# Amplitude product of kernel generation in two halves, with amplitudes in two tiles and new instruction sequences

## The chip, the cores and the metric

The kernel runs on one core of a Trainium2 chip. The core has a matrix engine (TensorE, PE in the profile, with its weight loads as PEld), three engines for elementwise work (VectorE, DVE; ScalarE, ACT; GpSimd, POOL) and a queue that issues the transfers (SyncE, SP). Each engine runs its own list of instructions in order and waits on semaphores for the others. The metric is the device time of one execution in microseconds, median of some runs.

## The reference

The input is a sequence of 2048 positions with 448 channels. Two branches work on it and a gate mixes them. Branch a is a state space model (S4D): per channel a convolution kernel K of length 2048 is generated from 256 complex modes, and the sequence is convolved with K by FFT. Branch b is a gated unit with 1792 features.

```python
x = A_u                                             # (1, 2048, 448)
g = sigmoid((x * gate_w).sum(-1, keepdims=True))

dt = exp(log_dt)
A = -exp(log_A_real) + 1j * A_imag                  # (448, 256)
C = (C_real + 1j * C_imag) * dt[:, None]
P = exp((A * dt[:, None])[:, :, None] * pos)        # (448, 256, 2048)
K = 2.0 * einsum("dn,dnl->dl", C, P).real           # kernel generation
y = irfft(rfft(x, 4096) * rfft(K, 4096))[:2048]
a = y + x * D_skip

b = (sigmoid(B_x_in @ w_gate) * (B_x_in @ w_up)) @ w_down    # B_x_in is x
out = g * a + (1 - g) * b
```

P would have 448 x 256 x 2048 entries; the kernel never forms it.

## The kernel before, in words

**Kernel generation.** A position is written as l = 32 a + b, and exp(A dt l) as a product of a factor in a and one in b, so that K is, per channel, a small matrix product over the modes. The 448 channels are worked in 28 chunks of 16 (`kgen`), the modes in two halves of 128, one on each partition: 56 half chunks. For each, `powers` lets POOL build tables of real powers (tile `tb`; L1212 sets ones, L1222 and L1225 multiply), and `half_chunk` makes the factors: PE computes phases in turns (L1232), ACT and PE take the whole turns off (L1236, L1238 and L1241), ACT makes sines and cosines (L1243, L1244, L1254) in the tile `cs` of 96 columns for each of sine and cosine and each of 16 channels. DVE makes the amplitudes `es` (96 columns) as two outer products of the small tables (L1261: 64 columns, 1024 elements a partition, then 32 columns, 512 elements) and multiplies them into cs: L1275 writes the columns 0 to 31 of cs from its columns 32 to 63 in reversed order and the first 32 of es (the part called n here, 1024 elements), and L1278 multiplies columns 32 to 95 in place by es 32 to 95 (2048 elements). `contract` then multiplies both half chunks of a chunk together on PE (L1290: 128 small matmuls of 32 columns), ACT takes the result out, and after 14 chunks the kernel of one half of the channels goes to memory for the FFT.

**The other work.** The gated unit runs for each of two halves of the positions in two blocks of 512. Its weights are split in two parts of less precision (`wh`, `wl`: ACT L1388, DVE or POOL L1390), so that one product is three matmuls (L1423 to L1425, and L1427, L1428 for the shorter last part) into PSUM tiles `gu`. ACT makes the tanh of the gate (L1407) and DVE the product (L1409, or L1412 and L1415 where it is split again into `hh` and `hl`). The down product goes to a PSUM tile `dn`, of which there is one (L1443; L1445 to L1447 where split), and from there into an output block `ob`: the first time by ACT (L1455) or DVE scaled by `og`, later by DVE adding (L1462). The gate's factors come from DVE: 16 dot products (L960), tanh on ACT, then `gs` = g (L964) and `og` = (1 - g)/2 (L966). FFT stages of the signal and of K are matmuls with DVE transposes and products between them.

**What sets the order.** The program lists its operations with what each reads and writes. A planner then emits them in an order that a table written into the kernel, `PLACE`, gives: for each engine, tile tag and priority a row of numbers, one for each operation, its place in that engine's list. Each engine's instructions run in the order of these places, SP's transfers too. A tile's buffers are handed out in rotation (`cs` 3, `tb` 2, `es` 1), so an operation that opens a new tile waits for the last user of the old one.

The lines of the diff, before:

## Time and profile before

| | us |
|---|---|
| runs | 687.88, 686.38, 685.76 (median 686.38) |
| profiled execution | 684.96 |
| its span, first to last instruction | 683.0 |
| PE busy | 669.7 (98%) |
| DVE busy | 603.7 (88%) |
| ACT busy | 509.7 (75%) |
| POOL busy | 269.2 (39%) |
| mean granted TensorE clock | 0.999 |

The busy time of an engine is the sum of what its instructions cover, so overlapping instructions count once. A row of a group has the line, the engine, the operation, what it writes and reads, the shapes and the count; behind the bars stand the total and mean time and the idle time of the engine before these instructions, with what ended it. A row of the timeline begins with start and duration in microseconds; brackets at its end give the idle time before it and its releaser. PE's matmuls are pipelined, so their records overlap by design. Kernel generation fills the stretch from about 75 to 500 us; the gated unit runs beside it all the time and alone with the second FFT chains after it.

### The profile page before, as it was taken

What the parts mean: (1) busy time and instruction counts of PE and PEld (TensorE: products, weight loads), DVE (VectorE), ACT (ScalarE), POOL (GpSimd) and SP (SyncE); (2) the same over time, 40 slices, a digit from 0 to 9 for tenths busy, and PEclk for the clock granted to TensorE, in tenths of its full rate; (3) what the DMA queues carried; (4) which work ended last, traced back from release to release, by engine and by line L of the source; (5) the groups of instructions that cost most, each with busy time, mean ns of one, the idle gap of its engine ahead of it and who ended that gap; (6) DMA issues with size and microseconds to landing.
All of it is one profiled execution on the core that took longest, in us unless ns stands there. A gap on an engine that the chain in (4) does not pass through costs nothing.

```text
span 683.0 us, 16235 instructions
## 1 busy us (share of the span) xinstructions
PE 669.7 (98%) x6568; PEld 480.6 (70%) x6568; DVE 603.7 (88%) x699; ACT 509.7 (75%) x928; POOL 269.2 (39%) x280
## 2 busy tenths in 40 slices
PE   8899999999999999999989999999999999999997
PEld 7677667877886687776646666778878766546864
DVE  7998999999899999999998999999974379667976
ACT  6588799898999999999999999999842442333110
POOL 0506486555466656675856567643000000000000
PEclk9999999999999999999999999999999999999999
DMA  8869432683793999737977884343968981888855
GB/s 265 222 146 245 111 101 57 174 217 139 208 173 85 204 203 225 237 111 178 176 211 179 200 212 113 124 155 111 204 133 217 280 292 66 300 276 217 153 141 129
DMA packets 96898, 122.79 MB, mean 180 GB/s; under 512 B 31032, under 2 KB 80504, under 8 KB 95800
## 3 DMA queue, kind: packets, MB, share of 16 engines
q1 hardware_dynamic: 96824, 121.76, 69.7%
q8 instruction: 52, 0.85, 0.5%
q14 instruction: 22, 0.18, 0.1%
HBM read 78.16 MB, written 43.58 MB: 178 GB/s over the span
## 4 chain that ended last, share of the span: by engine, by line
PE 82%; DVE 10%; ACT 3%; DMA 2%; issue 2%; SPq 1%; DVEq 0%
PE gu_gps L1423 10%; PE gu_gps L1424 9%; PE gu_gps L1425 9%; PE kp_egp L1290 7%; PE dn_gps L1443 6%; PE dn_gps L1445 5%; PE tp_egp L1232 4%; PE tp_egp L1241 4%; PE dn_gps L1446 4%; PE dn_gps L1447 4%; PE fps_fups L812 3%; PE gu_gps L1427 3%; PE fps_fups L845 3%; PE gu_gps L1428 3%; PE fps_fups L889 2%; PE fps_fkps L889 2%
## 5 line engine op out<-in xcount | busy, mean ns | idle before, releaser
L1423 PE MATMUL gu_gps<-xs_glu,wh_glu 128*128 128x512 f32 x336 | 144.6, 430 | 1.6 <-DVE hl_glu L1409 0.8
L1278 DVE TENSOR_TENSOR cs_eg<-cs_eg,es_eg 128x2048 f32<-128x2048 f32 x56 | 131.5, 2349 | 1.4
L1424 PE MATMUL gu_gps<-xs_glu,wh_glu 128*128 128x512 f32 x336 | 132.0, 393 | 0.1
L1425 PE MATMUL gu_gps<-xs_glu,wl_glu 128*128 128x512 f32 x336 | 131.7, 392 | 0.0
L1222 POOL TENSOR_TENSOR tb_eg<-tb_eg 128x96 f32<-128x96 f32 (+2 forms) x84 | 118.8, 1416 | 6.1
L1261 DVE TENSOR_TENSOR es_eg<-tb_eg 128x1024 f32<-128x1024 f32 x112 | 110.4, 1013 | 2.1 <-POOL tb_eg L1222 0.5
L1423 PEld LDWEIGHTS gu_gps<-xs_glu,wh_glu 128*128 128x128 f32 x336 | 63.2, 188 | 30.8 <-issue 15.8
L1275 DVE TENSOR_TENSOR cs_eg<-cs_eg,es_eg 128x1024 f32<-128x1024 f32 x56 | 70.8, 1264 | 8.2 <-ACT cs_eg L1254 5.8
L1238 ACT ACTIVATE nn_eg<-cs_eg 128x512 fp32r<-128x512 f32 x112 | 74.9, 669 | 3.8 <-PE tp_egp L1241 2.6
L1407 ACT ACTIVATE sg_glu<-gu_gps 128x512 f32<-128x512 f32 x56 | 34.5, 615 | 55.2 <-PE gu_gps L1428 54.9
L1424 PEld LDWEIGHTS gu_gps<-xs_glu,wh_glu 128*128 128x128 f32 x336 | 63.3, 188 | 16.0 <-issue 5.0
L1425 PEld LDWEIGHTS gu_gps<-xs_glu,wl_glu 128*128 128x128 f32 x336 | 63.1, 188 | 14.4
L1243 ACT ACTIVATE cs_eg<-tp_egp 128x512 f32<-128x512 f32 x112 | 70.0, 636 | 3.1 <-PE tp_egp L1241 2.7
L1236 ACT ACTIVATE cs_eg<-tp_egp 128x512 f32<-128x512 f32 x112 | 69.9, 633 | 2.7 <-PE tp_egp L1232 1.0
L1244 ACT ACTIVATE cs_eg<-tp_egp 128x512 f32<-128x512 f32 x112 | 69.0, 627 | 1.1 <-PE tp_egp L1241 1.1
L1254 ACT ACTIVATE cs_eg<-cs_eg,half_pi 128x1024 f32<-128x1024 f32 x56 | 66.7, 1191 | 0.2
L1225 POOL TENSOR_TENSOR tb_eg<-tb_eg,bs_eg 128x32 f32<-128x32 f32 x84 | 62.6, 745 | 6.4
L1462 DVE SCALAR_TENSOR_TENSOR ob_glu<-dn_gps,og,ob_glu 128x448 f32<-128x448 f32 x70 | 47.4, 677 | 16.0 <-PE dn_gps L1447 15.1
L1290 PEld LDWEIGHTS kp_egp<-cs_eg 128*32 128x32 f32 x3584 | 51.3, 110 | 10.7 <-issue 7.6
L1212 POOL MEMSET tb_eg<- 128x96 f32 x28 | 8.0, 287 | 127.9 <-DVE es_eg L1261 124.8
L1290 PE MATMUL kp_egp<-cs_eg 128*32 128x64 f32 x3584 | 55.8, 220 | 0.0
L1241 PE MATMUL tp_egp<-nn_eg,idn 128*128 128x512 f32 x112 | 51.4, 459 | 1.2 <-ACT nn_eg L1238 1.2
(168 smaller groups left out, 1326.0 us busy)
## 6 DMA issues: line engine op xcount, KB each, us to landing
shf<-fx_fu SPq DMA_DIRECT2D x16, 896.0 KB, 5.4
fx_fu<-shf SPq DMA_DIRECT2D x16, 896.0 KB, 10.4
us<-fx_fu SPq DMA_DIRECT2D x16, 896.0 KB, 9.7
xr_glu<-in_w_dram SPq DMA_DIRECT2D x46, 256.0 KB, 6.1
uax_fk<-us SPq DMA_DIRECT2D x16, 448.0 KB, 4.3
ua_fk<-us SPq DMA_DIRECT2D x16, 448.0 KB, 6.0
xr_glu<-in_w_dram SPq DMA_DIRECT2D x17, 224.0 KB, 4.1
gt_pre<-in_u_dram SPq DMA_DIRECT2D x8, 448.0 KB, 6.9
```

The lines of the kernel that those rows point to most:

```text
L1222: pool(96 * m, lambda n=n, m=m: G.tensor_mul(g3(n + 1, m), g3(1, m), g3(n, 1).to_broadcast([128, 32, 3, m])))
L1236: op("Act", c_act(512, True), lambda: S.activation(cs[:, 1, ds, 32:96], block(tp), AF.Copy, bias=MAGIC), [tp], [(cs, ("s", i))], prio)
L1238: op("Act", c_act(512), lambda: S.activation(block(nn), cs[:, 1, ds, 32:96], AF.Copy, scale=-1.0, bias=MAGIC), [(cs, ("s", i))], [nn], prio)
L1241: op("PE", c_mm(532), lambda: T.matmul(tp.real, idn.real, nn.real, start=False, stop=True, skip_group_check=True), [nn, idn], [tp], prio)
L1243: op("Act", c_act(512, True), lambda: S.activation(cs[:, 0, ds, 32:96], block(tp), AF.Abs), [tp], [(cs, ("c", i))], prio)
L1261: V.tensor_mul(o.rearrange("p d (i k) -> p d i k", k=ny), x.unsqueeze(3).to_broadcast([128, 16, nx, ny]), y.unsqueeze(2).to_broadcast([128 ...
L1275: op("DVE", c_dve(1024), lambda: V.tensor_mul(cs[:, :, :, 0:32], cs[:, ::-1, :, 63:31:-1], es[:, :, 0:32].unsqueeze(1).to_broadcast([128, ...
L1278: op("DVE", c_dve(2048), lambda: V.tensor_mul(cs[:, :, :, 32:96], cs[:, :, :, 32:96], es[:, :, 32:96].unsqueeze(1).to_broadcast([128, 2, 1 ...
L1290: T.matmul(kp[32 * j:32 * j + 32, q], cs[:, z, 4 * j + q, 64:96], cs[:, z, 4 * j + q, 0:64], start=cs is parts[0] and z == 0 and q == 0, s ...
L1423: T.matmul(p.real, wh[:, k, cs], x[:, k], start=(k == 0), stop=False)
L1424: T.matmul(p.real, wh[:, k, cs], x[:, 4 + k], start=False, stop=False)
L1425: T.matmul(p.real, wl[:, k, cs], x[:, k], start=False, stop=False)
```

## The change

Two things change. First, `half_chunk`: the amplitudes are now two tiles, `ea` for the first 64 columns and `es` (called eb in the code) for the last 32, one buffer each, of the same size together. The product of 2048 elements becomes two of 1024: f, columns 64 to 95 of cs by es (L1279), and m, columns 32 to 63 by the second half of ea (L1282). The part n (now L1276) reads the columns that m overwrites, so m comes after n; f needs neither. Lines below this part stand four further down in the changed kernel (L1423 is L1427 there), those above it two.

Second, `PLACE`: every row of it has new numbers, with 168 numbers for the operations on cs in place of 112 on DVE, and a row for ea. So the sequence of every engine is another, also where the operations are the same. The diff of the code, with the first numbers of the rows for cs as an example of the table:

```diff
-    ('DVE', 'cs', 20): (156, 158, 168, 169, 180, 186, 192, 193, 201, 202, 206, 208, 215, 217, 221, 223, 228, 229, 233,
...
+    ('DVE', 'cs', 20): (157, 156, 159, 166, 168, 171, 182, 192, 188, 193, 196, 195, 204, 205, 206, 210, 211, 212, 220,
...
@@ -1246,7 +1248,7 @@
 
     def half_chunk(c, nh, ph, tb, prio):
         cs = eg.tile("cs", CSB, (128, 2, 16, 96))
-        es = eg.tile("es", 1, (128, 16, 96))
+        ea, eb = eg.tile("ea", 1, (128, 16, 64)), eg.tile("es", 1, (128, 16, 32))
         for i in range(2):
             tp = egp.tile("tp", TPB, (128, 512))
             turns(c, nh, i, ph, cs, tp, prio)
@@ -1265,19 +1267,21 @@
         def r(k):
             tt = tb[:, q0:q0 + 16]
             if k == 0:
-                outer(es[:, :, 0:64], tt[:, :, 8:16], tt[:, :, 0:8])
+                outer(ea.real, tt[:, :, 8:16], tt[:, :, 0:8])
             else:
-                outer(es[:, :, 64:96], tt[:, :, 24:28], tt[:, :, 16:24])
+                outer(eb.real, tt[:, :, 24:28], tt[:, :, 16:24])
         for k in range(2):
-            op("DVE", c_dve(1024 - 512 * k), lambda k=k: r(k), [tb], [(es, 0), (es, 1)] if k == 0 else [(es, 2)], prio)
-
+            op("DVE", c_dve(1024 - 512 * k), lambda k=k: r(k), [tb], [ea] if k == 0 else [eb], prio)
 
         op("DVE", c_dve(1024), lambda: V.tensor_mul(
-            cs[:, :, :, 0:32], cs[:, ::-1, :, 63:31:-1], es[:, :, 0:32].unsqueeze(1).to_broadcast([128, 2, 16, 32])),
-           [*cos, *sin, (es, 0)], [(cs, "n")], prio)
-        op("DVE", c_dve(2048), lambda: V.tensor_mul(
-            cs[:, :, :, 32:96], cs[:, :, :, 32:96], es[:, :, 32:96].unsqueeze(1).to_broadcast([128, 2, 16, 64])),
-           [(es, 1), (es, 2)], cos + sin, prio)
+            cs[:, :, :, 0:32], cs[:, ::-1, :, 63:31:-1], ea[:, :, 0:32].unsqueeze(1).to_broadcast([128, 2, 16, 32])),
+           [*cos, *sin, ea], [(cs, "n")], prio)
+        op("DVE", c_dve(1024), lambda: V.tensor_mul(
+            cs[:, :, :, 64:96], cs[:, :, :, 64:96], eb.real.unsqueeze(1).to_broadcast([128, 2, 16, 32])),
+           [*cos, *sin, eb], [(cs, "f")], prio)
+        op("DVE", c_dve(1024), lambda: V.tensor_mul(
+            cs[:, :, :, 32:64], cs[:, :, :, 32:64], ea[:, :, 32:64].unsqueeze(1).to_broadcast([128, 2, 16, 32])),
+           [*cos, *sin, ea, (cs, "n")], [(cs, "m")], prio)
         return cs
 
     def contract(parts, kp, prio):
```

Three places show how the sequences move. The first is DVE in the middle of kernel generation, at the half chunks 17 and 18 (numbers behind a tile's name count its instances). L1415 and L1390 are splits of the gated unit, L1462 adds a down product. Before:

```order
L1275 TENSOR_TENSOR cs_eg17_2703<-cs_eg17_2703,es_eg17_2748 128x32x32
L1415 TENSOR_TENSOR hl_glu16_2805<-sg_glu21_2725,hh_glu16_2796 128x512
L1278 TENSOR_TENSOR cs_eg17_2703<-cs_eg17_2703,es_eg17_2748 128x32x64
L1390 TENSOR_TENSOR wl_glu12_2770<-xr_glu27_2158,wh_glu12_2690 128x512
L1261 TENSOR_TENSOR es_eg18_2903<-tb_eg9_2576 128x16x64
L1462 SCALAR_TENSOR_TENSOR ob_glu4_559<-dn_gps28_2751,og_76,ob_glu4_559 128x448
L1261 TENSOR_TENSOR es_eg18_2903<-tb_eg9_2576 128x16x32
L1275 TENSOR_TENSOR cs_eg18_2784<-cs_eg18_2784,es_eg18_2903 128x32x32
L1278 TENSOR_TENSOR cs_eg18_2784<-cs_eg18_2784,es_eg18_2903 128x32x64
L1261 TENSOR_TENSOR es_eg19_2952<-tb_eg9_2576 128x16x64
```

and with the change:

```order
L1279 TENSOR_TENSOR cs_eg17_2751<-cs_eg17_2751,es_eg17_2784 128x32x32
L1276 TENSOR_TENSOR cs_eg17_2751<-cs_eg17_2751,ea_eg17_2790 128x32x32
L1263 TENSOR_TENSOR es_eg18_2837<-tb_eg9_2595 128x512
L1419 TENSOR_TENSOR hl_glu16_2843<-sg_glu21_2742,hh_glu16_2820 128x512
L1282 TENSOR_TENSOR cs_eg17_2751<-cs_eg17_2751,ea_eg17_2790 128x32x32
L1263 TENSOR_TENSOR ea_eg18_2864<-tb_eg9_2595 128x1024
L1394 TENSOR_TENSOR wl_glu12_2755<-xr_glu27_2221,wh_glu12_2655 128x512
L1466 SCALAR_TENSOR_TENSOR ob_glu4_568<-dn_gps28_2803,og_76,ob_glu4_568 128x448
L1394 TENSOR_TENSOR wl_glu13_2947<-xr_glu28_2530,wh_glu13_2861 128x512
L1279 TENSOR_TENSOR cs_eg18_2812<-cs_eg18_2812,es_eg18_2837 128x32x32
L1276 TENSOR_TENSOR cs_eg18_2812<-cs_eg18_2812,ea_eg18_2864 128x32x32
L1282 TENSOR_TENSOR cs_eg18_2812<-cs_eg18_2812,ea_eg18_2864 128x32x32
```

Before, the 2048 product of one half chunk and the outer products of the next stand close together, with one other instruction between them or none. Now f comes first, then n; the outer product of 512 for the next half chunk stands right behind them, ahead of m, and the one of 1024 right behind m.

The second place is DVE in the head, where the factors gs and og of the first positions are made (L993 and L999 are work on the parameters of the state space model, L960 the dot products). Before:

```order
L1390 TENSOR_TENSOR wl_glu2_345<-xr_glu1_227,wh_glu2_299 128x512
L960 SCALAR_TENSOR_TENSOR gt_pre0_215,dots_pre0_359<-gt_pre0_215,gwb_pre0_225 128x448 x2
L1409 SCALAR_TENSOR_TENSOR hh_glu1_395<-sg_glu2_334,gu_gps5_328 128x512
L964 TENSOR_SCALAR gs_75<-dots_pre0_359 128x4
L993 TENSOR_SCALAR mx_pro0_290<-rt_pro1_281 112x512
L966 TENSOR_SCALAR og_76<-dots_pre0_359 128x4
L999 TENSOR_TENSOR mx_pro0_290<-mx_pro0_290,aci_pro0_263 112x512
```

and with the change:

```order
L1394 TENSOR_TENSOR wl_glu2_341<-xr_glu1_300,wh_glu2_310 128x512
L1413 SCALAR_TENSOR_TENSOR hh_glu1_383<-sg_glu2_339,gu_gps5_317 128x512
L962 SCALAR_TENSOR_TENSOR gt_pre0_215,dots_pre0_348<-gt_pre0_215,gwb_pre0_230 128x448 x2
L966 TENSOR_SCALAR gs_75<-dots_pre0_348 128x4
L968 TENSOR_SCALAR og_76<-dots_pre0_348 128x4
L995 TENSOR_SCALAR mx_pro0_273<-rt_pro1_280 112x512
L1001 TENSOR_TENSOR mx_pro0_273<-mx_pro0_273,aci_pro0_266 112x512
```

og stands right behind gs now, ahead of the instruction on mx; and hh1 stands ahead of the two dot products.

The third is PE in the head, at the second down product, dn_gps1. Before:

```order
L1427 MATMUL gu_gps7_381<-xs_glu1_229,wh_glu1_172 128x512
L1428 MATMUL gu_gps7_381<-xs_glu1_229,wl_glu1_189 128x512
L1423 MATMUL gu_gps8_407<-xs_glu0_126,wh_glu2_299 128x512
L1424 MATMUL gu_gps8_407<-xs_glu0_126,wh_glu2_299 128x512
L1425 MATMUL gu_gps8_407<-xs_glu0_126,wl_glu2_345 128x512
L1443 MATMUL dn_gps1_424<-vh_glu0_303,hh_glu0_231 128x448
L1443 MATMUL dn_gps1_424<-vh_glu1_322,hl_glu0_301 128x448
L1423 MATMUL gu_gps8_407<-xs_glu0_126,wh_glu2_299 128x512
L1424 MATMUL gu_gps8_407<-xs_glu0_126,wh_glu2_299 128x512
L1425 MATMUL gu_gps8_407<-xs_glu0_126,wl_glu2_345 128x512
```

and with the change:

```order
L1427 MATMUL gu_gps8_402<-xs_glu0_127,wh_glu2_310 128x512
L1428 MATMUL gu_gps8_402<-xs_glu0_127,wh_glu2_310 128x512
L1429 MATMUL gu_gps8_402<-xs_glu0_127,wl_glu2_341 128x512
L1427 MATMUL gu_gps8_402<-xs_glu0_127,wh_glu2_310 128x512
L1428 MATMUL gu_gps8_402<-xs_glu0_127,wh_glu2_310 128x512
L1429 MATMUL gu_gps8_402<-xs_glu0_127,wl_glu2_341 128x512
L1431 MATMUL gu_gps7_391<-xs_glu1_232,wh_glu1_171 128x512
L1432 MATMUL gu_gps7_391<-xs_glu1_232,wl_glu1_180 128x512
L1447 MATMUL dn_gps1_429<-vh_glu0_234,hh_glu0_236 128x448
L1447 MATMUL dn_gps1_429<-vh_glu1_315,hl_glu0_304 128x448
```

Here L1427 to L1429 of the change are L1423 to L1425 of before, and L1431 and L1432 are L1427 and L1428. The end of gu_gps7 moves behind the groups of gu_gps8. Over the whole list up to the second down product, what stands ahead of it is the same as before, and one more group of three on gu_gps8.

More of the change, by code (lines that the diff above doesn't have):

```diff
@@ L28 @@
 PLACE = {
-    ('Act', 'aci', 10): (14, 40,),
-    ('Act', 'aci', 19): (65, 94,),
-    ('Act', 'acr', 10): (15, 39, 49,),
-    ('Act', 'acr', 19): (63, 91, 101,),
[26 rows of a table removed]
-    ('Act', 'dots', 1): (28,),
-    ('Act', 'dots', 2): (45,),
-    ('Act', 'dots', 16): (67, 83,),
[18 rows of a table removed]
-    ('Act', 'idn', 10): (12,),
-    ('Act', 'junk', 10): (29, 60,),
-    ('Act', 'junk', 19): (77, 81, 132,),
[12 rows of a table removed]
-    ('Act', 'pos_sb', 10): (36, 52,),
[13 rows of a table removed]
+    ('Act', 'aci', 10): (15, 39,),
+    ('Act', 'aci', 19): (65, 95,),
+    ('Act', 'acr', 10): (14, 37, 52,),
@@ L109 @@
+    ('Act', 'acr', 19): (64, 92, 106,),
[26 rows of a table added]
+    ('Act', 'dots', 1): (30,),
+    ('Act', 'dots', 2): (45,),
+    ('Act', 'dots', 16): (68, 83,),
[18 rows of a table added]
+    ('Act', 'idn', 10): (11,),
+    ('Act', 'junk', 10): (32, 60,),
+    ('Act', 'junk', 19): (77, 81, 138,),
[12 rows of a table added]
+    ('Act', 'pos_sb', 10): (38, 40,),
[13 rows of a table added]
     ('Act', 'wh', 0): (1, 4,),
     ('Act', 'wh', 1): (6, 7,),
[4 rows of a table removed]
[4 rows of a table added]
     ('Act', 'xs', 0): (0, 2, 3, 5,),
[2 rows of a table removed]
-    ('DVE', 'aci', 10): (45,),
-    ('DVE', 'aci', 19): (122,),
[2 rows of a table added]
+    ('DVE', 'aci', 10): (41,),
+    ('DVE', 'aci', 19): (117,),
@@ L120 @@
     ('DVE', 'acr', 10): (89,),
-    ('DVE', 'acr', 19): (152,),
[1 row of a table removed]
+    ('DVE', 'acr', 19): (153,),
[1 row of a table added]
     ('DVE', 'ai', 19): (143,),
[3 rows of a table removed]
[3 rows of a table added]
     ('DVE', 'ci', 19): (140,),
[1 row of a table removed]
[1 row of a table added]
     ('DVE', 'cr', 19): (138, 141,),
[7 rows of a table removed]
-    ('DVE', 'dtp', 10): (30,),
-    ('DVE', 'dtv', 10): (27,),
[8 rows of a table removed]
[9 rows of a table added]
+    ('DVE', 'dtp', 10): (29,),
+    ('DVE', 'dtv', 10): (27,),
[8 rows of a table added]
     ('DVE', 'gs', 1): (53,),
[1 row of a table removed]
[1 row of a table added]
     ('DVE', 'gs', 16): (107, 126,),
[3 rows of a table removed]
-    ('DVE', 'half_pi', 0): (9,),
[24 rows of a table removed]
-    ('DVE', 'ones', 10): (1,),
-    ('DVE', 'p', 10): (18, 20, 21, 22, 23, 25, 26,),
@@ L180 @@
-    ('DVE', 'phs', 20): (2,),
[6 rows of a table removed]
-    ('DVE', 'skip', 20): (0,),
[6 rows of a table removed]
-    ('DVE', 'uax', 40): (539, 534, 546, 547, 556, 557, 570, 571, 578, 575, 585, 586, 590, 591, 595, 596, 624, 623,
[34 rows of a table removed]
[3 rows of a table added]
+    ('DVE', 'half_pi', 0): (1,),
[24 rows of a table added]
+    ('DVE', 'ones', 10): (3,),
+    ('DVE', 'p', 10): (18, 19, 20, 22, 23, 25, 26,),
+    ('DVE', 'phs', 20): (0,),
[6 rows of a table added]
+    ('DVE', 'skip', 20): (2,),
[6 rows of a table added]
+    ('DVE', 'uax', 40): (596, 593, 603, 602, 614, 612, 625, 624, 631, 634, 642, 641, 646, 647, 654, 653, 678, 679,
[34 rows of a table added]
         1039,),
[2 rows of a table removed]
[2 rows of a table added]
         1041,),
[39 rows of a table removed]
[39 rows of a table added]
```

520 rows, old and new, of the table PLACE are left out of this document.

## The prediction

> **What bounds the kernel now.** I read the page first: what PE does, and who owns the chain that ended last.
>
> ```profile
> span 683.0 us, 16235 instructions
> PE 669.7 (98%) x6568; PEld 480.6 (70%) x6568; DVE 603.7 (88%) x699; ACT 509.7 (75%) x928; POOL 269.2 (39%) x280
> PE 82%; DVE 10%; ACT 3%; DMA 2%; issue 2%; SPq 1%; DVEq 0%
> ```
>
> PE (TensorE) is busy 98% and owns 82% of the chain. DVE owns 10%, though it is busy 88%: it is near the bound, not the bound. So I read next where PE still idles, and how far DVE is from the bound while kernel generation runs. That is the table by stage; its columns are start and end, then length, PE, PEld, DVE, ACT and POOL busy, clock, DMA share and GB/s.
>
> ```profile
> 0.00:100.00 100.00, 94.56 (x371) 68.15 (x372) 92.12 (x179) 75.92 (x134) 41.63 (x42) 1.00 0.70 184
> 100.00:320.00 220.00, 220.00 (x2674) 164.18 (x2673) 213.30 (x207) 210.17 (x383) 130.70 (x134) 1.00 0.67 169
> 320.00:360.00 40.00, 37.85 (x619) 23.32 (x621) 39.44 (x35) 37.94 (x69) 30.34 (x29) 1.00 0.88 191
> 360.00:500.00 140.00, 139.98 (x1718) 103.94 (x1707) 130.80 (x118) 134.57 (x249) 66.56 (x77) 1.00 0.65 161
> 500.00:640.00 140.00, 140.00 (x975) 94.28 (x975) 95.09 (x105) 47.31 (x91) 0.00 (x0) 1.00 0.79 224
> 640.00:683.00 43.00, 37.26 (x232) 26.77 (x230) 32.94 (x60) 3.79 (x7) 0.00 (x0) 0.99 0.57 131
> ```
>
> PE idles 683.0 - 669.7 = 13.3 us: 5.44 in the head (0 to 100), 2.15 between 320 and 360, 5.74 at the end, 0.02 elsewhere. Not all of it can move. The end is drain: the last matmul row is
>
> ```profile
> 677.86 0.37 PE L1447 MATMUL gu_gps<-vl_glu,hh_glu 128*128 128x448 f32 x1
> PE fps_fups L1039 <- DVE ones_pro L1034: 1.2, 1, 1.2
> ```
>
> so 683.0 - 678.2 = 4.8 us follow PE, and the second row (the waits: total, count, longest) is 1.2 us before PE's first matmul. That leaves 13.3 - 4.8 - 1.2 = 7.3 us that an order of work could take away, about 1.1% of the time. DVE in the stages of kernel generation (100 to 500) is busy 213.30 + 39.44 + 130.80 = 383.5 of 400, so 16.5 us are left to it; ACT is busy 382.7, so 17.3 us are left. These three numbers, 7.3, 16.5 and 17.3, are what the change is weighed against.
>
> **The split of the product on DVE.** The amplitude work of one of the 56 half chunks now is four DVE instructions (columns: total us, mean ns, idle before):
>
> ```profile
> L1278 DVE TENSOR_TENSOR cs_eg<-cs_eg,es_eg 128x2048 f32<-128x2048 f32 x56 | 131.5, 2349 | 1.4
> L1261 DVE TENSOR_TENSOR es_eg<-tb_eg 128x1024 f32<-128x1024 f32 x56 | 72.3, 1291 | 2.1 <-POOL tb_eg L1222 0.5
> L1275 DVE TENSOR_TENSOR cs_eg<-cs_eg,es_eg 128x1024 f32<-128x1024 f32 x56 | 70.8, 1264 | 8.2 <-ACT cs_eg L1254 5.8 <-ACT cs_eg L1244 2.1
> L1261 DVE TENSOR_TENSOR es_eg<-tb_eg 128x512 f32<-128x512 f32 x56 | 41.1, 734 | 0.0
> ```
>
> The change cuts the 2048 product into two of 1024. The nearest row for such a half is L1275, the same operation on 1024 elements. By the records a split costs 2 x 1264 - 2349 = 179 ns, times 56 = 10.0 us of DVE. That is the upper bound. But records of neighbours overlap, and by how much depends on whether the second reads what the first wrote:
>
> ```profile
> 491.03 1.22 DVE L1275 TENSOR_TENSOR cs_eg<-cs_eg,es_eg 128x1024 f32<-128x1024 f32 x1
> 492.16 0.68 DVE L1462 SCALAR_TENSOR_TENSOR ob_glu<-dn_gps,og,ob_glu 128x448 f32<-128x448 f32 x1
> 492.76 0.68 DVE L1261 TENSOR_TENSOR es_eg<-tb_eg 128x512 f32<-128x512 f32 x1
> 493.47 2.29 DVE L1278 TENSOR_TENSOR cs_eg<-cs_eg,es_eg 128x2048 f32<-128x2048 f32 x1
> ```
>
> L1462 starts 0.09 us before L1275 ends, and the 512 outer product 0.08 before L1462 ends: these pairs are independent. L1278 reads the es just written and starts 0.03 after its end. So an independent instruction costs its record less 0.08, and a dependent pair costs 0.11 more than that. A split then is 0.179 - 0.08 = 0.10 us, times 56 = 5.6 us. Against it the new order pulls producers and consumers apart. I counted in DVE's sequence the neighbours of which the second needs the first: 71 before (37 n to the rest of the product, 30 that product to the next outer product, 4 outer to product), 37 after. 34 fewer at 0.11 give back 3.7 us. Net on DVE: +1.9 us; bounds -0.1 (the added instructions cost little) and +10.0 (full records, nothing given back). I take +1.9, since the overlap is in the rows above.
>
> The Trainium skill, "VectorE: DVE Perf Modes", section "The DRAIN you can't avoid", speaks against this: it says that the next operation does not start before the pipe is empty, and that a semaphore between two costs nothing, so that one should save instructions, not waits. The trace here disagrees in the small (0.08 before the end against 0.03 after it); by that page the sum on DVE would be the full 10.0 us, and it is the second rival below. The 0.10 us per split stands near the 75 ns per instruction of "Vector Engine (DVE) Microarchitecture Reference", section "5.2 Measured stream behaviour on trn2"; an estimate from that page alone would be 56 x 75 ns = 4.2 us.
>
> What hides it: DVE has 16.5 us left in 100 to 500, where PE idles only 2.2. So +1.9 on DVE costs **0** on the path. What waits is arranged anew: the next outer products waited both for the 2048 product (one es tile, one buffer); now that of 512 into es waits only for the far product f, and that of 1024 into ea for n and m, of which m also stands behind n. All of these are DVE's own, so nothing of another engine is queued behind a new wait but the contraction. If the cover goes, what lies behind a late product is L1290, the contraction on PE, and behind a late outer product POOL's next powers table.
>
> **ACT.** Its instruction rows are the same; their order changes.
>
> ```profile
> 490.44 0.60 ACT L1236 ACTIVATE cs_eg<-tp_egp 128x512 f32<-128x512 f32 x1 [0.67 <-PE kp_egp L1290]
> 491.06 0.63 ACT L1238 ACTIVATE nn_eg<-cs_eg 128x512 fp32r<-128x512 f32 x1
> ```
>
> L1238 reads what L1236 wrote and starts 0.02 after it. In ACT's sequence such neighbours (L1236 to L1238, L1243 to L1254) rise from 42 to 52. No quoted ACT pair is independent, so I price the rise by DVE's 0.11: 10 x 0.11 = 1.1 us, between 0 and twice that. ACT has 17.3 us left: **0** on the path.
>
> **PE.** Its instructions are the same in number and kind. What can change is where it switches between full and tiled matmuls:
>
> ```profile
> 501.31 0.40 PE L1425 MATMUL gu_gps<-xs_glu,wl_glu 128*128 128x512 f32 x1
> 501.64 0.98 PE L845 MATMUL fps_fups<-fx_fu,m_sb 64*64 64x448 f32 x8
> 502.55 1.99 PE L1290 MATMUL kp_egp<-cs_eg 128*32 128x64 f32 x128
> 504.48 0.50 PE L1427 MATMUL gu_gps<-xs_glu,wh_glu 128*128 128x512 f32 x1
> 504.81 0.40 PE L1428 MATMUL gu_gps<-xs_glu,wl_glu 128*128 128x512 f32 x1
> 505.05 0.39 PE L1427 MATMUL gu_gps<-xs_glu,wh_glu 128*128 128x512 f32 x1
> ```
>
> Two full matmuls in a row end 505.44 - 505.21 = 0.23 us apart; the first after a tiled block ends 504.98 - 504.54 = 0.44 after it. So a switch costs 0.2 us. In the sequences I count 177 switches before and 175 after: 2 x 0.2 = **-0.4 us**. The end of the program is in the same order: 0 there.
>
> **The head, where PE waits.** Rows of PE, with idle time and releaser in brackets:
>
> ```profile
> 29.32 1.02 PE L1443 MATMUL dn_gps<-vh_glu,hl_glu 128*128 128x448 f32 x2 [0.45 <-DMA vh_glu<-in_w_dram]
> 30.95 0.50 PE L1423 MATMUL gu_gps<-xs_glu,wh_glu 128*128 128x512 f32 x1 [0.61 <-DVE hh_glu L1409]
> 34.11 1.02 PE L1443 MATMUL dn_gps<-vh_glu,hh_glu 128*128 128x448 f32 x2 [1.05 <-ACT ob_glu L1455]
> ```
>
> and the work that releases them:
>
> ```profile
> 30.22 0.68 DVE L1409 SCALAR_TENSOR_TENSOR hh_glu<-sg_glu,gu_gps 128x512 f32<-128x512 f32 x1
> 30.82 1.15 DVE L964 TENSOR_SCALAR gs<-dots_pre 128x4 f32<-128x4 f32 x1
> 31.89 0.41 DVE L993 TENSOR_SCALAR mx_pro<-rt_pro 112x512 f32<-112x512 f32 x1
> 32.22 1.11 DVE L966 TENSOR_SCALAR og<-dots_pre 128x4 f32<-128x4 f32 x1
> 33.43 0.63 ACT L1455 ACTIVATE ob_glu<-dn_gps,og 128x448 f32<-128x448 f32 x1 [1.37 <-DVE og L966]
> ```
>
> The second down product waits for its single PSUM buffer, that for ACT's first output block, that for og on DVE. The change moves three things here. L993 goes behind og, so og comes 32.22 - 31.89 = 0.33 us sooner. One more group of three gate matmuls stands ahead of that down product on PE: 3 x 0.23 = 0.69 us of work in place of waiting. Together 1.02 of the 1.05. And hh (L1409) moves ahead of two dot products on DVE, so the 0.61 at 30.95 goes; but it only brings PE sooner to the same down product, whose wait grows by as much. So the sum is 0.61 + 1.05 - (0.61 + 0.03) = 1.02, **-1.0 us**. What could take it back: the weights vh of the second feature block are needed 11 rows of PE earlier (some 2.4 us), while SP's queue has 0.48 MB less ahead of them, 0.48 MB / 184 GB/s = 2.6 us. These cancel; bounds +/-0.5, about the 0.45 at 29.32.
>
> **The other waits.** They lie in the head at 75.41 and 89.36, and in the middle:
>
> ```profile
> 75.41 1.02 PE L1443 MATMUL dn_gps<-vh_glu,hh_glu 128*128 128x448 f32 x2 [0.77 <-DVE ob_glu L1462]
> 89.36 1.02 PE L1443 MATMUL dn_gps<-vh_glu,hl_glu 128*128 128x448 f32 x2 [0.52 <-DVE ob_glu L1462]
> 342.75 0.50 PE L1241 MATMUL tp_egp<-nn_eg,idn 128*128 128x512 f32 x1 [1.21 <-ACT nn_eg L1238]
> 347.40 0.50 PE L1423 MATMUL gu_gps<-xs_glu,wh_glu 128*128 128x512 f32 x1 [0.85 <-DVE hl_glu L1409]
> ```
>
> Every sequence differs there, and I cannot follow from an order whether such a wait closes, stays or opens elsewhere. Bounds: all of it gone, -(0.77 + 0.52 + 2.15) = -3.4; or once more as much, +3.4. I take **+0.3**, a little to the bad, since waits like 1.21 and 0.85 belong to the old order's few loose places and a new order has its own.
>
> Sum: 0 + 0 - 0.4 - 1.0 + 0.3 = -1.1 us. The profiled execution took 684.96 (span 683.0 and 1.96 around it), the median of the runs is 686.38, 1.42 above it. So 683.9 for a profiled execution, and 686.38 - 1.1 = **685.3** for the median.
>
> **The rivals.** *First, the new order closes most waits.* The dn wait (1.0), the middle (2.15) and the switches (0.4) go: -3.55, so 686.38 - 3.5 = 682.9. For it: two half products of 1024 let the product on the far half of the turns start without the whole amplitude tile, and dependent neighbours on DVE halve. Against it: PE shows 0.02 us of idle in all of 100 to 320 and 360 to 640, so there is nothing to win in most of the span.
>
> *Second, slower: DVE becomes the bound in kernel generation.* The place is the stretch where half chunks follow each other, 100 to 500; the price is the full record, 10.0 us; it decides when the new work exceeds what of DVE's 16.5 idle us can be used. If half of it, 8.2, is usable (the other half lies in waits for ACT, as the 8.2 us before L1275 show), that is from 383.5 + 8.2 = 391.7 us of DVE in these stages on. Then 10.0 - 8.2 = 1.8 us come through, and ACT's chain behind it adds its 1.1, some +3: 689.4. For it: DVE at 97% between 100 and 320. Against it: the overlap in the timeline and the 34 handovers saved.
>
> *Third, the new order runs into waits of its own* at another place, as at 34.11, 75.41 and 347.40 now: three such (1.05 + 0.77 + 0.85) are +2.7: 689.1. For it: every engine's sequence is new. Against it: counted in PE's sequence, its stages (last contraction, first transforms, products) move by at most 1.4 us of work.
>
> **How the numbers follow.** Near neutral, my forecast: 0.45. The first rival 0.28, the second 0.12, the third 0.15. About 0.3%, 2.06 us, is what a measurement of this kernel can tell from no change. The forecast's own range is 683.0 to 687.6: 2.3 to either side, two thirds of the 3.4 of the other waits gone, or as much added. With the rivals the range is 681.5 to 689.5: the first rival with another 1.4 closed, the second with its 689.4. Faster than 684.32: most of the first rival and a fifth of the forecast, 0.27 + 0.09 = 0.36. Slower than 688.44: most of the second and third with a small part of the forecast, 0.21. Same: 0.43.
>
> **What would show it.** Right: DVE busy in 100 to 500 up by some 2 to 10 us with PE still at 220.0 of 220; the halves at about 1.26 us; the two waits at 30.95 and 34.11, 1.66 now, down to some 0.65; PE's busy sum within 1 us of 669.7. Wrong: PE idle in 100 to 320 above 1 us before L1290 with DVE as releaser (second rival); new waits of over 0.7 us in the head or middle (third); the middle's 2.15 gone (first).

## The result

| | runs | median us | ratio to the kernel before, 95% interval |
|---|---|---|---|
| before | 6 | 688.56 (685.76 to 689.97) | |
| changed | 6 | 692.9 (691.48 to 694.0) | 1.007 [1.0045, 1.0096] |
| changed, run again | 10 | 691.72 (687.8 to 694.33) | 1.0048 [1.0016, 1.008] |

The change makes the kernel 0.5 to 0.7% slower, 3.6 to 4.3 us by the medians; forecast were 685.3 and 1.1 us less than before. The page of the changed kernel (engines' busy time, then the chain that ended last) and its table by stage:

```profile
span 691.0 us, 16276 instructions
PE 670.8 (97%) x6568; PEld 481.2 (70%) x6568; DVE 608.5 (88%) x755; ACT 510.1 (74%) x928; POOL 247.7 (36%) x280
PE 66%; DVE 14%; DMA 9%; ACT 5%; issue 3%; SPq 2%; POOL 2%; DVEq 0%; ACTq 0%
...
0.00:100.00 100.00, 96.61 (x384) 69.73 (x384) 92.80 (x180) 76.24 (x137) 37.39 (x41) 1.00 0.67 182
100.00:320.00 220.00, 214.39 (x2651) 160.53 (x2649) 212.01 (x232) 205.88 (x374) 121.49 (x134) 1.00 0.63 165
320.00:360.00 40.00, 37.58 (x506) 23.40 (x504) 39.49 (x41) 37.66 (x69) 25.22 (x30) 1.00 0.93 202
360.00:500.00 140.00, 139.67 (x1812) 102.57 (x1811) 131.56 (x136) 135.82 (x250) 63.64 (x78) 1.00 0.63 161
500.00:640.00 140.00, 137.52 (x960) 91.97 (x959) 92.18 (x104) 49.22 (x94) 0.00 (x0) 1.00 0.78 219
640.00:691.00 51.00, 44.99 (x266) 33.02 (x264) 40.46 (x67) 5.26 (x9) 0.00 (x0) 0.98 0.64 136
```

PE's busy time is 1.1 us more, its idle time 691.0 - 670.8 = 20.2 us in place of 13.3. By stage: 3.4 in the head (5.4 before), **5.6 between 100 and 320 (0.0 before)**, 2.4 in the middle (2.2), 0.3 to 500, **2.5 between 500 and 640 (0.0 before)**, 6.0 at the end (5.7). The chain says the same in other words: the transfers' share rose from 2 to 9%. These are the rows of PE behind the two new numbers and the middle:

```profile
206.51 0.98 PE L847 MATMUL fps_fups<-fx_fu,m_sb 64*64 64x448 f32 x6 [1.03 <-DMA fx_fu<-shf]
246.18 0.70 PE L1234 MATMUL tp_egp<-pos_sb,phs 97*128 97x512 f32 x2 [0.68 <-DMA phs<-phd]
251.89 1.54 PE L1294 MATMUL kp_egp<-cs_eg 128*32 128x64 f32 x95
256.52 0.66 PE L1294 MATMUL kp_egp<-cs_eg 128*32 128x64 f32 x33 [3.09 <-issue]
291.14 0.80 PE L814 MATMUL fps_fups<-fx_fu,ft_fu 64*128 64x224 f32 x5 [0.65 <-DMA ft_fu<-in_s1t_dram]
350.41 0.50 PE L1427 MATMUL gu_gps<-xs_glu,wh_glu 128*128 128x512 f32 x1 [1.28 <-DVE hh_glu L1413]
548.89 0.93 PE L814 MATMUL fps_fkps<-fx_fk,ft_fk 64*128 64x224 f32 x6 [2.34 <-DMA fx_fk<-kd]
```

Four waits between 100 and 320 make 5.45 of the 5.6. Three are for transfers. The largest, 3.09 us, stands in the middle of one contraction, after 95 of its 128 matmuls, and waits for nothing that the profile shows ("issue"). The 2.34 us at 548.9 is for a load of K.

**The kernel before has the same gap in another execution.** Its second profile, 687.76 us (span 685.9), where the first had 684.96:

```profile
252.80 1.11 PE L1290 MATMUL kp_egp<-cs_eg 128*32 128x64 f32 x63
255.69 0.64 PE L1290 MATMUL kp_egp<-cs_eg 128*32 128x64 f32 x29 [1.77 <-issue]
```

The profile on which the prediction rests was one of the fastest executions: medians of before over 6 to 25 runs are 688.2 to 690.0.

**DVE.** The three products of the changed kernel by group:

```profile
L1276 DVE TENSOR_TENSOR cs_eg<-cs_eg,ea_eg 128x1024 f32<-128x1024 f32 x56 | 72.0, 1286 | 2.3 <-ACT cs_eg L1256 1.7 <-ACT cs_eg L1246 0.4
L1279 DVE TENSOR_TENSOR cs_eg<-cs_eg,es_eg 128x1024 f32<-128x1024 f32 x56 | 72.0, 1285 | 5.1 <-ACT cs_eg L1256 3.9 <-PE gu_gps L1429 0.5 <-ACT cs_eg L1238 0.5
L1282 DVE TENSOR_TENSOR cs_eg<-cs_eg,ea_eg 128x1024 f32<-128x1024 f32 x56 | 71.0, 1267 | 0.7
```

f and m take 1.285 + 1.267 us where one instruction took 2.349; DVE's busy time rose by 608.5 - 603.7 = 4.8 us (607.5 - 603.5 = 4.0 between the second profiles), between the 1.9 that were taken and the bound of 10.0.

### The profile page after: what moved, and what is told of

Read it like the earlier page. It is cut to its first block, busy times and chain, and to the rows that moved or that the text cites. A ratio compares the mean times of both kernels' runs of the same rounds, so it can differ in the third digit from the quotient of the medians.

```text
span 691.0 us, 16276 instructions
## 1 busy us (share of the span) xinstructions
PE 670.8 (97%) x6568; PEld 481.2 (70%) x6568; DVE 608.5 (88%) x755; ACT 510.1 (74%) x928; POOL 247.7 (36%) x280
## 4 chain that ended last, share of the span: by engine, by line
PE 66%; DVE 14%; DMA 9%; ACT 5%; issue 3%; SPq 2%; POOL 2%; DVEq 0%; ACTq 0%
PE gu_gps L1427 8%; PE gu_gps L1428 7%; PE gu_gps L1429 7%; PE dn_gps L1447 6%; PE kp_egp L1294 6%; PE tp_egp L1234 3%; PE dn_gps L1449 3%; PE fps_fups L814 3%; PE dn_gps L1450 3%; PE tp_egp L1243 3%; PE dn_gps L1451 3%; PE fps_fups L847 3%; PE gu_gps L1431 2%; PE gu_gps L1432 2%; PE fps_fkps L891 2%
## 5 line engine op out<-in xcount | busy, mean ns | idle before, releaser
L1427 PE MATMUL gu_gps<-xs_glu,wh_glu 128*128 128x512 f32 x336 | 142.4, 424 | 1.8 <-DVE hh_glu L1413 1.5
L1428 PE MATMUL gu_gps<-xs_glu,wh_glu 128*128 128x512 f32 x336 | 132.1, 393 | 0.0
L1429 PE MATMUL gu_gps<-xs_glu,wl_glu 128*128 128x512 f32 x336 | 131.8, 392 | 0.0
L1224 POOL TENSOR_TENSOR tb_eg<-tb_eg 128x192 f32<-128x192 f32 (+2 forms) x84 | 97.0, 1156 | 6.2
L1427 PEld LDWEIGHTS gu_gps<-xs_glu,wh_glu 128*128 128x128 f32 x336 | 63.2, 188 | 28.3 <-issue 11.9
L1279 DVE TENSOR_TENSOR cs_eg<-cs_eg,es_eg 128x1024 f32<-128x1024 f32 x56 | 72.0, 1285 | 5.1 <-ACT cs_eg L1256 3.9
L1240 ACT ACTIVATE nn_eg<-cs_eg 128x512 fp32r<-128x512 f32 x112 | 73.0, 652 | 3.2 <-PE tp_egp L1243 2.1
L1238 ACT ACTIVATE cs_eg<-tp_egp 128x512 f32<-128x512 f32 x112 | 68.7, 621 | 8.0 <-PE tp_egp L1234 5.8
L1276 DVE TENSOR_TENSOR cs_eg<-cs_eg,ea_eg 128x1024 f32<-128x1024 f32 x56 | 72.0, 1286 | 2.3 <-ACT cs_eg L1256 1.7
L1428 PEld LDWEIGHTS gu_gps<-xs_glu,wh_glu 128*128 128x128 f32 x336 | 63.3, 188 | 15.4 <-issue 3.9
L1227 POOL TENSOR_TENSOR tb_eg<-tb_eg,bs_eg 128x32 f32<-128x32 f32 x84 | 71.4, 851 | 5.9
L1429 PEld LDWEIGHTS gu_gps<-xs_glu,wl_glu 128*128 128x128 f32 x336 | 63.1, 188 | 14.4
L1282 DVE TENSOR_TENSOR cs_eg<-cs_eg,ea_eg 128x1024 f32<-128x1024 f32 x56 | 71.0, 1267 | 0.7
L1263 DVE TENSOR_TENSOR ea_eg<-tb_eg 128x1024 f32<-128x1024 f32 x56 | 70.1, 1252 | 0.4
L1245 ACT ACTIVATE cs_eg<-tp_egp 128x512 f32<-128x512 f32 x112 | 68.6, 621 | 2.0 <-PE tp_egp L1243 1.4
L1246 ACT ACTIVATE cs_eg<-tp_egp 128x512 f32<-128x512 f32 x112 | 68.5, 619 | 1.0 <-PE tp_egp L1243 0.8
L1294 PEld LDWEIGHTS kp_egp<-cs_eg 128*32 128x32 f32 x3584 | 51.4, 110 | 13.3 <-issue 9.5
```

Source lines behind the costliest of these rows:

```text
L1224: pool(96 * m, lambda n=n, m=m: G.tensor_mul(g3(n + 1, m), g3(1, m), g3(n, 1).to_broadcast([128, 32, 3, m])))
L1227: pool(32, lambda e=e: G.tensor_mul(t(e + 1), t(e), b(3)))
L1238: op("Act", c_act(512, True), lambda: S.activation(cs[:, 1, ds, 32:96], block(tp), AF.Copy, bias=MAGIC), [tp], [(cs, ("s", i))], prio)
L1240: op("Act", c_act(512), lambda: S.activation(block(nn), cs[:, 1, ds, 32:96], AF.Copy, scale=-1.0, bias=MAGIC), [(cs, ("s", i))], [nn], prio)
L1263: V.tensor_mul(o.rearrange("p d (i k) -> p d i k", k=ny), x.unsqueeze(3).to_broadcast([128, 16, nx, ny]), y.unsqueeze(2).to_broadcast([128 ...
L1276: op("DVE", c_dve(1024), lambda: V.tensor_mul(cs[:, :, :, 0:32], cs[:, ::-1, :, 63:31:-1], ea[:, :, 0:32].unsqueeze(1).to_broadcast([128, ...
```

## The experiments

Two theories stood against each other. **A:** the new sequences run into waits on transfers and into that gap, and the cut is covered (this part of it is later called O). **B** (later D): the added DVE time costs time itself. All ratios are to runs of the kernel before on the same chip; the experiments ran on three chips, so a ratio of one chip beside that of another is a weaker comparison than two on the same.

**The two parts one by one: e1_split_alone, e2_order_alone.** The first is the kernel before with

```diff
-        op("DVE", c_dve(2048), lambda: V.tensor_mul(
-            cs[:, :, :, 32:96], cs[:, :, :, 32:96], es[:, :, 32:96].unsqueeze(1).to_broadcast([128, 2, 16, 64])),
-           [(es, 1), (es, 2)], cos + sin, prio)
+        def halves():
+            V.tensor_mul(cs[:, :, :, 64:96], cs[:, :, :, 64:96], es[:, :, 64:96].unsqueeze(1).to_broadcast([128, 2, 16, 32]))
+            V.tensor_mul(cs[:, :, :, 32:64], cs[:, :, :, 32:64], es[:, :, 32:64].unsqueeze(1).to_broadcast([128, 2, 16, 32]))
+        op("DVE", c_dve(2048), halves, [(es, 1), (es, 2)], cos + sin, prio)
```

> The kernel before with its old sequences and one amplitude tile; only the product of 2048 is cut into two of 1024, issued one behind the other. Theory A (the 4 us come from waits on transfers and on PE's code fetch that the new sequences run into, the split is covered by DVE's 16.5 idle us): within 1 us of the kernel before, DVE busy in 100 to 500 up by 5 to 10 us, PE idle there unchanged. Rival B (the 56 added DVE instructions make DVE the bound): 2 to 6 us slower than the kernel before.

The second is the changed kernel with one amplitude tile; both outer products stand at the place of the larger one, the whole product at the place of m, and the places of f and of the small outer product stay empty:

```diff
-        ea, eb = eg.tile("ea", 1, (128, 16, 64)), eg.tile("es", 1, (128, 16, 32))
+        ea, eb = eg.tile("ea", 1, (128, 16, 96)), Res(name="es", real=0)
...
-        for k in range(2):
-            op("DVE", c_dve(1024 - 512 * k), lambda k=k: r(k), [tb], [ea] if k == 0 else [eb], prio)
+        op("DVE", c_dve(1024) + c_dve(512), lambda: (r(0), r(1)), [tb], [ea], prio)
...
+        op("DVE", c_dve(2048), lambda: V.tensor_mul(
+            cs[:, :, :, 32:96], cs[:, :, :, 32:96], ea[:, :, 32:96].unsqueeze(1).to_broadcast([128, 2, 16, 64])),
+           [*cos, *sin, ea, (cs, "n")], [(cs, "m")], prio)
```

> The changed kernel with its new sequences on every engine, but the product of 2048 whole (at the place of the last half, m) and both outer products into one tile, issued at the place of the larger one. Theory A: as slow as the changed kernel, 3 to 8 us above the kernel before, with PE waiting in 200 to 300 for transfers (some 2.4 us) and within a contraction for nothing shown (some 3 us), and at 549 for the load of K (2.3 us). Rival B: the loss is gone, within 1 us of the kernel before.

Measured: the cut alone 1.0086 [1.0054, 1.0119], the order alone 1.0022 [0.9992, 1.0052]. That is B, at first sight: the cut costs some 6 us in the old sequences, where A had at most 1. The order alone cannot be told from no change; A had 3 to 8 us for it. Two rows and two stretches of e1 show where its time goes (the stretches with PE, PEld, DVE, ACT, POOL busy and then the granted clock):

```profile
256.31 0.64 PE L1291 MATMUL kp_egp<-cs_eg 128*32 128x64 f32 x29 [2.42 <-issue]
353.34 0.51 PE L1424 MATMUL gu_gps<-xs_glu,wh_glu 128*128 128x512 f32 x1 [2.13 <-DVE hl_glu L1410]
...
350.00:353.30 3.30, 1.21 (x27) 0.64 (x15) 3.27 (x5) 2.20 (x4) 2.68 (x5) 1.00 0.00 0
353.30:357.00 3.70, 3.66 (x13) 1.46 (x14) 3.70 (x5) 1.30 (x3) 0.00 (x0) 0.57 0.66 173
```

DVE is later, and the wait for hl, 0.85 in the kernel before, is 2.13. Behind it PE's granted clock is 0.57 for 3.7 us: the records behind the profile give one stretch of 3.41 us at half clock, another 1.7 us lost. "TensorE: Matmul & The Clock Gate" of the Trainium skill, part 1, tells of windows of 3413 ns and a half clock; it puts the drop after an idle window of that length, and here 2.1 us of wait were enough. The four slowest executions of e1 have mean clocks of 0.989 to 0.993 at 696 to 700 us, the fastest 0.997 at 691.

So DVE's 16.5 idle us do not cover the cut by themselves. But e2's profile has the gap (2.47) and the wait for K (2.47) as well, without any added DVE instruction; these belong to the order, as A has it.

**The gap inside the contraction: e3_fetch_shift, e6_fetch_early, e7_before_fetch, e11_stores_later.** The trace has transfers of 16 KB on the queue for instructions, 52 in an execution, about one for 256 of PE's instructions. The thought was that the one PE needs near 254 comes late, since it stands behind three stores of 896 KB. e3 changes the warm-up:

```diff
-                T.matmul(wake[:, :128], ones.real, ones.real, start=True, stop=True)
+                T.matmul(wake[:, :64], ones.real, ones[:, :64], start=True, stop=True)
+                T.matmul(wake[:, 64:128], ones.real, ones[:, 64:], start=True, stop=True)
```

> The changed kernel with each of the 14 warm-up matmuls of 128 columns at the start cut into two of 64: PE's instruction list is 112 instructions longer ahead of the first real matmul, at about the same time for them, so every later boundary of its code fetches (16 KB, 256 instructions) falls 112 instructions earlier in the work. Theory A: the fetch that began at 254.1 in the changed kernel, behind three stores of 896 KB issued from 242.5 on, now begins before them near 239, the 3.09 us gap inside the contraction at 256.5 is gone, and the time is 2 to 3.5 us lower than the changed kernel's, if no other fetch falls into a burst. Rival C (the gap has another cause, such as a late operand or a dropped record): the gap stays and the time is the changed kernel's within 1 us.

Measured: 1.011 [1.0062, 1.0158]. The time is a miss, for a reason of the edit's own: a record of 64 columns took as long as one of 128 or longer (0.21 against 0.18 us), and the first real matmul began at 13.78 us where it began at 6.85. (They are 28 more records, so 56 instructions with their loads, not 112.) The gap near 256 is gone; PE stood still for nothing shown at other places, the longest 1.86 us at 352.9. So a cheaper edit, for the changed kernel (e6) and the kernel before (e7):

```diff
                 T.matmul(wake[:, :128], ones.real, ones.real, start=True, stop=True)
+            for _ in range(6):
+                T.matmul(wake[0:32, :64], ones[:, :32], ones[:, :64], start=True, stop=True)
```

> The changed kernel with six very small matmuls (32 by 64) added behind the warm-up matmuls at the start: PE's list is 12 to 24 instructions longer there, so that each later code fetch is due that much earlier in the work; the one near 243 us would be due near 240 to 241, ahead of the three stores issued from 242.5 on. Theory A: the gap of 2 to 3 us inside a contraction near 255 is gone, no start later than 0.5 us, and the time is 1.5 to 3 us lower than the changed kernel's (ratio about 1.003 to 1.005). Rival: the gap stays, or gaps as long appear at other contractions; 1.006 to 1.008.

> The kernel before with the same six small matmuls behind its warm-up. Theory A (its own executions lose up to 1.8 us in the same contraction near 255, when the fetch comes behind the three stores): that gap is gone in the profile, and the median falls by 1 to 2 us (ratio 0.997 to 0.9985). Rival: no difference, within 0.5 us.

Measured: 1.0013 [0.9987, 1.004] for the changed kernel with it, 0.9969 [0.9946, 0.9991] for the kernel before with it. The same contraction in e6, unbroken:

```profile
251.56 1.99 PE L1296 MATMUL kp_egp<-cs_eg 128*32 128x64 f32 x128
253.48 0.50 PE L1429 MATMUL gu_gps<-xs_glu,wh_glu 128*128 128x512 f32 x1
```

Twelve short matmul records at the start, and by the ratios both kernels are 2 to 4 us faster. For the changed kernel that compares chips, since it was not run without the edit on the chip of e6; e4 below, on that chip and without the edit, has 690.14 against 688.98. The pair says one thing more: on one chip, both with the edit, the changed kernel is still slower than the kernel before, 688.98 against 687.05 us (1.0013 against 0.9969). The gap is a loss that both kernels have, and a good part of their difference, 2 to 3 us, is left when it is gone. e11 leaves PE's list alone and moves two of the stores in SP's list (sp) behind the next load of bs:

```diff
+        for _ in range(2):
+            sp.insert(143, sp.pop(141))
```

> The changed kernel with two of the three stores of 896 KB issued from 242.5 us on moved behind the next table load (bs) in SP's queue, which was issued at 255.5; PE's list is untouched. Theory A (the code fetch that PE needs near 254 waits behind those stores): the fetch begins before 250 and the gap near 256 is gone or under 0.7 us in the profile; ratio to the kernel before 1.000 to 1.004 where the changed kernel had 1.005 to 1.007. Rival (the stores are not what holds the fetch): the gap stays at 2 to 3 us.

Measured: the fetch began at 249.4 and the gap is gone, as A said. It began just as the data of the one store left ahead of it ran out; from then to 256 the DMA share is 0.01. The time, 1.0107 [1.0075, 1.014], is a miss. The later stores hold up the loads of signal behind them in SP's queue, ACT waits for one of these, and PE for ACT:

```profile
272.18 0.63 ACT L1360 ACTIVATE xs_glu<-xr_glu 128x512 fp32r<-128x512 f32 x1 [4.52 <-DMA xr_glu<-in_ut_dram]
274.01 0.50 PE L1249 MATMUL tp_egp<-nn_eg,idn 128*128 128x512 f32 x1 [4.03 <-ACT nn_eg L1246]
```

Read from the transfers of all profiles (us; the first store is that of the burst, the fetch the 16 KB transfer that PE needs at its instruction 4488 or so):

```
kernel                  first store  fetch begins  gap in the contraction
before, first profile        242.8         243.4    none
before_again                 244.1         253.2    1.77
changed                      242.5         254.1    3.09
after_again                  242.1         254.0    3.19
e1_split_alone               244.0         254.1    2.42
e2_order_alone               242.3         252.3    2.47
e4_kd_earlier                243.9         244.5    none
e5_split_at_m                243.5         253.2    1.94
e10_split_alone_fetch        246.1         256.2    3.00
e6, e7, e8, e9, e12          242.3 to 243.0   240.9 to 242.2   none
e3_fetch_shift               248.5         246.0    none
e11_stores_later             243.7 (one)   249.4    none
```

Where the fetch begins before the first store or at most 0.7 us behind it, there is no gap. Else, with three stores ahead, it begins 9 to 12 us behind the first, and PE waits 1.8 to 3.2 us, in all seven at its instruction 4488: it has run out of instructions. Where nothing held it, the fetch began at instruction 4228 to 4258 (two counted for a matmul record, the weight load with it). With PE's list as it was, PE came to 4228 in nine profiles 0.6 to 0.8 us behind the issue of the first store; in two of them (before, e4) the fetch got through, in six it was held behind three stores, and in e11 behind one. What decides between them is not seen. "Runtime: NRT & Kernel Launch" of the Trainium skill, section "Instruction fetch mechanics", has the 16 KiB blocks of 256 instructions and calls their cost mostly hidden. So it is here: of the 52 fetches of an execution this is the only one with such a gap, but for e3, e6 and e9, which have some of 0.7 to 1.9 us near 350 and 380.

**The load of K: e4_kd_earlier, e8_fetch_and_kd.** e4 is the changed kernel with one load moved in SP's list:

```diff
+        sp.insert(279, sp.pop(282))
```

> The changed kernel with one transfer moved three places up in SP's queue: the load of a part of K (fx_fk from kd) that PE waited 2.34 us for at 548.9 is issued ahead of a load of 448 KB of signal spectra, a weight load and a table load. Theory A (the new SP order puts it too late): the wait falls below 0.5 us, and the time is 2 to 4 us lower than the changed kernel's (ratio to the kernel before about 1.003). Rival (the transfers are the bound there, 105% of the engines' share): another wait of PE on a transfer, of 1.5 us or more, appears between 540 and 565 and the time stays at 1.006 to 1.008.

Measured: 1.0004 [0.997, 1.0038]; but the wait is still 1.83 us at 546.58, so the lower time is not shown to come from it (the fetch got through in this profile). That wait differs much from one profile to the next: 0.55 and 2.34 us in the changed kernel, 2.47, 2.20, 3.03, 1.64 and 0.43 in e2, e3, e5, e6 and e9. e8 moves three loads and adds the six small matmuls:

```diff
+        for a, b in ((277, 276), (278, 277), (282, 278)):
+            sp.insert(b, sp.pop(a))
```

> The changed kernel with the six small matmuls behind the warm-up and with three loads of K moved up in SP's queue, ahead of two loads of signal spectra of 448 KB, a weight load and a table. Theory A (both waits are placed by the new sequences and can be taken away singly): no gap near 255, the wait for fx_fk near 546 under 0.7 us; ratio 0.997 to 1.000, 1 to 2 us below the run with the fetch alone. Rival (transfers bound that stretch): the fx_fk wait stays above 1.3 us or its time turns up at ua_fk or uax_fk; ratio as with the fetch alone, 1.000 to 1.003.

Measured: **0.9967 [0.9945, 0.999]**, the fastest of the changed kernels: 5.5 us below the changed kernel on the same chip (686.25 against 691.72), and by the ratio 3 us below e6, which ran on another. The wait is gone, and PE idles nowhere between 360 and 640:

```profile
span 682.7 us, 16299 instructions
...
542.28 1.03 PE L820 MATMUL fps_fkps<-fx_fk,ft_fk 64*128 64x224 f32 x8
...
360.00:500.00 140.00, 140.00 (x1689) 104.44 (x1689) 132.18 (x139) 135.90 (x250) 58.95 (x74) 1.00 0.65 166
500.00:640.00 140.00, 140.00 (x975) 94.55 (x974) 95.08 (x104) 45.96 (x88) 0.00 (x0) 1.00 0.78 225
```

So the transfers were not the bound there; their order was.

**The cut, with the gap out of the way: e9_order_alone_fetch, e10_split_alone_fetch, e12_order_fetch_kd.** e9 and e10 are e2 and e1 with the six small matmuls; e12 is e9 with the three loads of K moved as in e8.

> The new sequences with the product whole, and the six small matmuls. With the fetch out of the way in all four, the parts can be told apart: both parts gave 1.0013, neither 0.9969. Theory D (the cut costs time, the order alone little): 0.997 to 0.999. Theory O (the order's later waits cost, the cut nothing): 1.000 to 1.003.

> The old sequences with the product cut in two, and the six small matmuls. Theory D: 1.002 to 1.007, as the split alone without them less the fetch, with PE waiting longer than in the kernel before for what DVE makes (hl, ob) between 320 and 360. Theory O: 0.996 to 0.999, as the kernel before with them.

> The new sequences with the product whole, the six small matmuls behind the warm-up, and the three loads of K moved up: the run that had 0.9967 with the cut product, without the cut. Theory D (the cut costs some of DVE's 9 us also here): 0.992 to 0.995. Theory O (in the new sequences the cut is covered): 0.996 to 0.999.

| with the small matmuls | product whole | product cut |
|---|---|---|
| old sequences | 0.9969 [0.9946, 0.9991] | 1.0152 [1.0103, 1.0201] |
| new sequences | 1.0004 [0.9975, 1.0033] | 1.0013 [0.9987, 1.004] |
| new sequences, loads of K moved | 0.9972 [0.9939, 1.0005] | 0.9967 [0.9945, 0.999] |

In the new sequences the cut costs nothing that can be measured (1.0004 and 1.0013; 0.9972 and 0.9967), though DVE is busy 606.1 against 601.9 us in the last pair, 4.2 us for 56 cuts. That is O; D's 0.992 to 0.995 for e12 lies below the 0.9972, though the interval reaches to 0.9939. In the old ones it costs 1.8%, a late fetch included. The 1.0152 is more than either theory had: the small matmuls did not help there, and the fetch came late again (3.00 at 258.57, with a stretch at half clock), beside the wait for hl (2.11 at 357.15, with another). Why it came late is open: PE passed its instruction 4246 at 245.15, 0.96 us ahead of the first store, just as in e7 (241.57 and 242.53), and still the fetch began 10.1 us behind that store. The fetch ahead of it was late too, at PE's instruction 4230 where e7 has 4034.

**Where the halves stand: e5_split_at_m.** The new sequences, as e2, but with the cut, both halves at m's place:

```diff
-        op("DVE", c_dve(2048), lambda: V.tensor_mul(
-            cs[:, :, :, 32:96], cs[:, :, :, 32:96], ea[:, :, 32:96].unsqueeze(1).to_broadcast([128, 2, 16, 64])),
+        op("DVE", c_dve(2048), halves,
            [*cos, *sin, ea, (cs, "n")], [(cs, "m")], prio)
```

> The new sequences with the product cut in two halves, but both halves issued one behind the other at the place of m, and both outer products at the place of the larger one, into one tile: against the run with the whole product in these sequences, only the cut differs. Theory D (the added DVE time of some 9 us costs time itself, as the split alone in the old order did): the ratio is that of the changed kernel, 1.006 to 1.010. Rival (in the new order the cut is covered, the rest is order): 1.001 to 1.004, as with the whole product.

Measured: 1.0105 [1.0053, 1.0158], beside 1.0022 for e2 (on another chip), so the cut costs here too, as D said. The changed kernel has the same instructions and 1.005 to 1.007; what it adds is f and the small outer product at their own, earlier places, with a tile of their own. In e5 DVE is late for PE again (row of PE: a down product waiting for DVE's addition):

```profile
327.52 0.64 PE L1447 MATMUL dn_gps<-vh_glu,hl_glu 128*128 128x448 f32 x1 [1.73 <-DVE ob_glu L1466]
```

It has also the gap (1.94) and 3.03 us of wait for K, with three stretches at half clock, so how much of its time the place of f is worth by itself is not settled.

**The same kernels once more: after_again, before_again.**

> The changed kernel once more, on one chip with the next three and with the kernel before. Theory A (a code fetch behind stores, in some executions and not in others, is a good part of the difference): ratio to the kernel before 1.004 to 1.008, executions spread over 4 us or more, and the gap inside the contraction near 255 is there or not there with a difference of 2 to 3 us. Rival: 1.007 again with all executions close together.

> The kernel before once more, for its profile beside those of this chip. Theory A: PE's idle time is as in the first profile, 13 to 14 us; if this execution is some 3 us longer, one gap of PE of about 3 us without a releaser shows it (a code fetch late here too). Otherwise the span is 683 to 684.

Measured: 1.0048 [1.0016, 1.008] with executions from 687.8 to 694.3; its profile has the gap, 3.19 at 256.38, and only 0.55 of wait for K. before_again is the second profile of before shown with the result. Between these two profiles of one chip, PE idles 2.2 us less in the head and 2.7 us more between 100 and 320, 1.7 us more between 360 and 500 (ACT late for L1234 at 496.69).

## Why the prediction was wrong

*"Every sequence differs there ... I take +0.3."* This step failed. The term of the other waits was bounded by the size of the waits in before's trace (0.77, 0.52, 2.15), all for DVE and ACT in the head and the middle, and where PE had no idle time, nothing was added. It came to +5.6 us between 100 and 320 and +2.5 between 500 and 640 in the profile (2.34 of it one wait), for transfers and a code fetch. The first trace has one wait of PE on a transfer (0.45 at 29.32) and none on a code fetch. The third rival (new waits of its own, "three such", +2.7, chance 0.15) was the nearest, though its waits were again those for DVE and ACT. The late code fetch and the load of K account for the loss: without them the changed kernel goes from 1.005 to 1.007 to 1.0013 (e6) and 0.9967 (e8). But the kernel before gains from the same six matmuls, to 0.9969 (e7), so the difference between the two kernels lies for a good part in the loads of K; with them moved as well, e8 is level with e7. How the loads do it is shown less well than that they do: in e9's profile the wait for K is only 0.43 us, and e12 with the loads moved is still at 0.9972 against 1.0004, with intervals that overlap. The two parts are not separated to the microsecond, since the intervals are some 2 us wide to either side. The profile sums to more than the medians do (span +8.0 us; medians +3.6 to +4.3; the two second profiles +4.0), because of the next point.

*"The profiled execution took 684.96 ... the median of the runs is 686.38"*. The sum was made against an execution in which the fetch began 0.67 us behind the first store and was not held. Of the 1.4 us between it and the median nothing was asked; before_again shows a gap of 1.77 us in it. 220.00 busy of 220.00 was taken for the kernel's state, and it is one of two that its two profiles show.

*"So +1.9 on DVE costs 0 on the path."* The 0 is right in the changed kernel (e6 against e9, e8 against e12), the 1.9 is not: DVE's busy time rose by 4.0 to 4.8 us. The term that was mis-sized is the cut, 0.10 us each: in e1, where every handover of the old order stays, 56 cuts cost 612.5 - 603.5 = 9 us, 0.16 each. The changed kernel has 4 to 5 us less than that, of the size of the 3.7 that were taken for the saved handovers, but nothing was run that changes these alone. The sign "up by some 2 to 10 us" between 100 and 500 did not come (383.1 against 383.5): with PE's stops the work ran later, and 40.5 us of DVE's stood behind 640 where 32.9 had been. In e8, without the stops, DVE has 389.0 between 100 and 500. And the reason given, 16.5 us of idle time as a cover, does not hold by itself: in the old sequences the 9 us cost some 6 (e1), the second rival's mechanism in part. The gap of 3.09 us stands at the contraction, where that rival's sign was to be seen, but without DVE as releaser. What covers the cut in the new sequences is argued, not shown: the order in which f, n, m and the outer products stand among the other work, or the second tile.

*The head, -1.0 us.* Right in kind and too small: neither wait, at 30.95 and 34.11, is left, and the head's idle time fell from 5.4 to 3.4 us, or 6.2 to 4.0 between the second profiles. *"-0.4 us"* for two switches cannot be seen: PE's busy time rose by 1.1 us between the first profiles and fell by 0.3 between the second. *ACT, 0 on the path,* held between 100 and 320; the 1.73 us at 496.69 in after_again is ACT's.
